# Splitting the projection of v over the two row halves of TensorE

## The chip, the cores and the metric

The kernel runs on one core of a Trainium2 chip. The metric is the time of one execution on the device, in microseconds; lower is better. The engines are TensorE (PE, with its weight loads as PEld), VectorE (DVE), ScalarE (ACT), GpSimd (POOL) and SyncE (SP), which issues transfers.

## The reference

With S = 2048 rows, D = 512, 32 heads of 16 and 688 gate channels, the kernel computes, from `xn = layernorm(x)`, the sum of `x` and two branches:

```
q, k, v = split(xn @ wqkv)                        # 32 heads of 16
pq, pk  = q @ w_phi, k @ w_phi                    # per head
phi(p)  = concat(softmax(p), softmax(-p))         # 32 features per head
kv, z   = phi(pk)^T v, sum over s of phi(pk)
o       = (phi(pq) kv) / (phi(pq) z + 1e-6)
A       = o @ wo

y       = gelu(xn @ w_in)                         # 2 x 688 channels
z1, z2  = y[:688], layernorm(y[688:])
B       = (z1 * (w_sp @ z2 + b_sp)) @ w_out

out     = x + A + B
```

## The kernel before, in words

All matmul products of accuracy are made of three: each operand is split into a high part `h` (rounded to the type float32r) and a rest `l`, and `mm3` adds `ah bh`, `ah bl` and `al bh` into the same PSUM bank (lines 51, 52, 53).

The first stage goes over 16 tiles of 128 rows of x. For a tile `s` the rows are centred, transposed on TensorE (`transposed`, line 248, into a tile `pt`) and split into `xT[s]`, whose first 512 columns in each of two slices hold the high part and the rest, as four chunks of 128 contraction rows by 128 tokens. Then there are three projections from the same `xT[s]`: `proj_k` and `proj_q` (weights folded with the feature map beforehand, in the matmuls `fold` of line 197) and `proj_v`. Each is `proj`: four chunks of three matmuls with 128 contraction rows, 128 output partitions and 512 columns, all into one PSUM tile named `proj`, which is one bank. k and q go through `softmax_pair`: four VectorE operations that read `proj` (lines 103, 104, 108, 109), an exponential on ScalarE (line 110), a sum and a reciprocal (lines 112, 113). v is evacuated by one ScalarE activation that scales each row (line 257). `add_kv` (lines 267 to 274) multiplies the features of k (line 269) and accumulates `kvps`, 16 small matmuls per tile of 32 output partitions and 64 columns, each of two instructions, over all 16 tiles.

The PSUM tiles of this stage are `kv_ps` with 2 banks, `za` with 2 and `p0ps` with 4 (tag "mm"); the 4 are shared by `proj` of k, q and v and by the transposes. v has two buffers in SBUF, so v of tile s + 2 is written when `kvps` of tile s has read its own. While the stage runs, matmuls named `zps` (two sums of twelve matmuls with 344 columns per tile) make the gate's first half (`z1_raw`, lines 136 to 140); they use the banks of `za`.

The order of the first two tiles is written out by hand (lines 296 to 339: `keep` puts an instruction into the order of its engine). From tile 0's `add_kv` on, the loop of line 341 gives an order of priority only: `proj_k(s)`, the transposes of `s + 2`, `proj_q`, `add_kv(s)`, `proj_v(s + 2)`, then `zps`. A planner that simulates the engines puts every engine's instructions in order, and may bring forward later work whose inputs are ready. On the chip each engine then keeps to that order.

Later stages make the second half of the gate, the large product with `w_sp` (matmuls named `g`), and the output: `po` (line 761, 64 output partitions, 256 columns) and `pout`.

Of the kernel before, what the change touches and what calls it, by code (L numbers as in the profile page):

```python
# [10 lines left out]
F32 = mybir.dt.float32  # L11
F32R = mybir.dt.float32r
AF = mybir.ActivationFunctionType
ALU = mybir.AluOpType
# [4 lines left out]
P = 128  # L19
S, D, H, DH, FH = 2048, 512, 32, 16, 688  # L20
NT = S // P
ND = D // P
# [9 lines left out]
HP, QP = P // 2, P // 4  # L32
# [3 lines left out]
def mixer(ctx: ExitStack, tc: tile.TileContext, x, x_t, wv, wqkT, phi_bd, wo, w_in, wst, b_r, w_out, out):  # L36
    nc = tc.nc
    pe, act, dve, pool, sp = nc.tensor, nc.scalar, nc.vector, nc.gpsimd, nc.sync
# [10 lines left out]
    def mm3(dst, a, b, start, stop):  # L49
        (ah, al), (bh, bl) = a, b  # L50
        pe.matmul(dst, ah, bh, start=start, stop=False)  # L51
        pe.matmul(dst, ah, bl, start=False, stop=False)  # L52
        return pe.matmul(dst, al, bh, start=False, stop=stop).ins  # L53
# [25 lines left out]
    r_x = cst.tile([P, NT], F32, name="r_x")  # L79
# [42 lines left out]
    def zproj(ps, s, w, order=(0, 1)):  # L122

        if ps in (za, kv_ps_p):
            p = [ps.tile([P, D], F32, tag="z", name="zps") for _ in range(2)]
        else:
            q = ps.tile([P, 2, D], F32, tag="z", name="zps")
            p = [q[:, k] for k in range(2)]
        t = xT[s]
        for k, j in enumerate(order):  # L130
            for c in range(ND):
                cs = slice(c * P, (c + 1) * P)
                mm3(p[k][:, :FC], (t[:, 0, cs], t[:, 1, cs]), (w[j][0][:, c], w[j][1][:, c]), c == 0, c == ND - 1)
        return [(slice(k, k + 1), p[k][:, :FC].unsqueeze(1)) for k in range(2)] if ps in (za, kv_ps_p) else [(slice(0, 2), q[:, :, :FC])]
# [8 lines left out]
    xT = []  # L143
# [17 lines left out]
    with ExitStack() as p0:  # L161
        res = p0.enter_context(left("p0res", 1))
        wk = p0.enter_context(left("p0wk", 2))
        ps = p0.enter_context(psum("p0ps", 4))
# [6 lines left out]
        wv_h = res.tile([P, ND, D], F32R, name="wv_h")  # L171
        wv_l = res.tile([P, ND, D], F32R, name="wv_l")
# [40 lines left out]
        def proj(s, wh, wl):  # L213
            p = ps.tile([P, D], F32, tag="mm", name="proj")
            for c in range(ND):
                cs = slice(c * P, (c + 1) * P)
                proj.last = mm3(p, (xT[s][:, 0, cs], xT[s][:, 1, cs]), (wh[:, c], wl[:, c]), c == 0, c == ND - 1)
            return p

        xt, v = {}, {}  # L220

        def fetch(s):
# [31 lines left out]

        def proj_v(s):
            v[s] = wk.tile([P, D], F32, tag="v", name="v")
            ins = act.activation(v[s], proj(s, wv_h, wv_l), AF.Copy, scale=r_x[:, s:s + 1]).ins
            return proj.last, ins

        def proj_k(s):  # L260
# [35 lines left out]
        with ExitStack() as queue:  # L296
# [22 lines left out]
            p = proj(0, wqk_h[:, 1], wqk_l[:, 1])  # L319
# [6 lines left out]
            keep(dve=i, act=center(2, nm))  # L326
            ek = softmax_pair(wk, p, "k", r_x[:, 0:1])
            keep(pe=proj_v(0)[0])
            for k in range(2):
                accs = [(2 * k + m, za.tile([P, D], F32, tag="z", name="fold")) for m in range(2)]  # L330
                for g in range(NG):
                    i = fold(wqT, g, accs)
                folded(0, accs)
                if k == 0:
                    keep(pe=i)
                    pt, i = transposed(2)
                    keep(pe=i)
                    split_x(pt)
                    proj_v(1)
        n1 = nq = 0  # L340
        for s in range(NT):
            fetch(s + 4)
            er = proj_k(s) if s else ek
            if 0 < s < NT - 2:
                centered(s + 2)
            while nq < (s - 2) * NT // (NT - 3):
                proj_q(nq)
                nq += 1
            add_kv(s, er)
            if s + 2 < NT:  # L350
                proj_v(s + 2)
            if s == 1:
                for j in range(2):
                    load_win(w1[j], j, wk, "x", XB)
            while n1 < s * (NT - LAG) // (NT - 1):
                z1_raw(wk, za, n1, 2)
                n1 += 1
# [18 lines left out]
    def q_fin(et, tmp, zb):  # L376

        e, r, t, w = et[:, :NF], *(et[:, NF + k * 2 * H:NF + (k + 1) * 2 * H] for k in range(3))
        den = et[:, NF + 6 * H:QW]
        dve.tensor_tensor(tmp, e, zb, op=ALU.mult)  # L380
        dve.tensor_reduce(t, heads(tmp), axis=AX.X, op=ALU.add)
        dve.tensor_tensor(t, t, r, op=ALU.mult)
        dve.scalar_tensor_tensor(den, pairs(t, 0), EPS_DEN, pairs(t, 1), op0=ALU.add, op1=ALU.add)
        dve.reciprocal(den, den)
        dve.tensor_tensor(w.rearrange("p (h a) -> p h a", a=2), r.rearrange("p (h a) -> p h a", a=2),
                          den.unsqueeze(2).to_broadcast([P, H, 2]), op=ALU.mult)
        return e, dve.tensor_tensor(heads(e), heads(e), bc(w, 2 * H), op=ALU.mult).ins
# [46 lines left out]
    with ExitStack() as p1:  # L434
# [39 lines left out]
        for s in range(NE):  # L474
            et = load_q(s, tb.tile([P, QW], F32, tag="et", bufs=2, name="et"))
            tmp = zw.tile([P, 4, FC], F32, tag="z2", bufs=2, name="qtmp").rearrange("p a b -> p (a b)")[:, :NF]
            e, _ = q_fin(et, tmp, zb)
# [56 lines left out]
    for s in range(NT):  # L534
        p = zproj((kv_ps_p, zc, zbp, za)[s % 4], s, w2, (0, 1) if s % 2 == 0 else (1, 0))
# [4 lines left out]
        for k, q in p:  # L540
            ins = act.activation(z[:, k], q, AF.Gelu_apprx_tanh, scale=r_x[:, s:s + 1]).ins
# [6 lines left out]
        r = zw.tile([P, 1], F32, tag="rstd", bufs=2, name="rstd")  # L548
# [206 lines left out]
    def attend(fs):  # L755

        oT = [wk.tile([P, NG, 2 * P], F32R, tag=f"oT{k}", name="oT") for k in "hl"]
        po = [pso.tile([P, 2, 2 * P], F32, tag="po", bufs=2, name="po") for _ in range(2)]
        for g in range(NG):
            for a in range(2):  # L760
                lasts[3] = pe.matmul(po[g // 2][a * HP:(a + 1) * HP, g % 2], kvT[:, 2 * g + a], fs[g][:, a],  # L761
                                     start=True, stop=True).ins
        for k in range(2):
            gs = slice(2 * k, 2 * k + 2)
            round_h(act, oT[0][:, gs], po[k])
            ins = rest_l(oT[1][:, gs], po[k], oT[0][:, gs])
        return oT, ins

    def project_u(i, u):
        uh, ul, rt = u  # L770
        p = pso.tile([P, D], F32, tag="out", bufs=2, name="pout")
        for c in range(KF):
            mm3(p, (uh[:, c], ul[:, c]), wu[c], c == 0, False)
        for w in wu[KF]:
            pe.matmul(p, rt, w, start=False, stop=False)
        return p
# [13 lines left out]
    p = {0: project_u(0, uT.pop(0))}  # L790
# [5 lines left out]
    oT, ins = attend(fT)  # L796
# [14 lines left out]
    for i in range(0, NT, 2):  # L811
        if i:
# [3 lines left out]
            with tc.issue_after(lasts[2]):  # L816
                oT, _ = attend(fT)
# [49 lines left out]
```

## Time and profile before

| | |
|---|---|
| time, median of 2 runs | 655.19 us (654.72 and 655.67) |
| span of the profiled execution | 651.5 us |
| time of the profiled execution outside its span | not given by the profile; the median is 3.7 us above the span |
| TensorE busy | 644.0 us, 99% of the span |
| VectorE busy | 509.3 us, 78% |
| ScalarE busy | 279.4 us, 43% |
| first stage with its 16 tiles | to about 215 us of the span |

A row of the groups of instructions gives line, engine, operation, written tile <- read tiles, shapes and count, then busy time and mean duration in ns, then idle time ahead of it and its cause. The duration of a matmul runs from its start to the end of its passage through the array; consecutive matmuls overlap, so what one costs in a dense stretch is the distance between two starts. In the chain of work that ended last, the second number of a row is the time that the step added to the chain. A row of waits gives what waited, for whom, the microseconds in total, the number of times and the longest. In the forms, `128*64` is the number of array rows and columns that a matmul uses.

### The profile page before, as it was taken

The page shows a single profiled execution, that of the slowest core. Times are in us where ns is not written, and L with a number is a line of the kernel's source. Part 1 is how long each engine was busy: PE and PEld are TensorE (multiplying, and loading weights), DVE is VectorE, ACT ScalarE, POOL GpSimd, SP SyncE. Part 2 cuts the span into 40 slices and gives each one's busy share as a digit, 9 for nine tenths or more (in the row PEclk, how much of TensorE's full clock was granted, in tenths as well). Part 3 has the DMA queues.
Part 4 walks back from the last instruction along what each step waited for, and adds up shares of the span by engine and source line. Part 5 has one row for each costly group of instructions (what it writes and reads, how often), then busy time and mean ns, then how long its engine had stood idle before and what let it go on. Part 6 is the DMA issues. An engine that isn't in the chain of part 4 may idle for free.

```text
span 651.5 us, 10927 instructions
## 1 busy us (share of the span) xinstructions
PE 644.0 (99%) x4163; PEld 580.2 (89%) x4163; DVE 509.3 (78%) x921; ACT 279.4 (43%) x464; POOL 96.6 (15%) x185
## 2 busy tenths in 40 slices
PE   7999999999999999999999999999999999999997
PEld 6888888888888999999999999999999777787885
DVE  4988987998889578989977869678696588989321
ACT  5644334342333438887443434434452432233220
POOL 3332221101101014441010010010100000001000
PEclk9999999999999999999999999999999999999999
DMA  8365344544444951002353352433557867864610
GB/s 307 78 161 138 100 130 103 149 124 113 124 141 144 302 164 65 2 2 78 129 187 128 124 171 89 163 122 115 177 182 269 290 210 265 295 237 165 214 50 32
DMA packets 38884, 98.36 MB, mean 151 GB/s; under 512 B 4688, under 2 KB 6736, under 8 KB 38832
## 3 DMA queue, kind: packets, MB, share of 16 engines
q1 hardware_dynamic: 27632, 56.77, 26.7%
q0 software_dynamic: 8896, 35.26, 17.8%
q10 hardware_dynamic: 2304, 5.64, 2.3%
q8 instruction: 32, 0.52, 0.3%
q14 instruction: 20, 0.16, 0.1%
HBM read 56.37 MB, written 26.61 MB: 127 GB/s over the span
## 4 chain that ended last, share of the span: by engine, by line
PE 97%; DMA 1%; DVE 0%; ACT 0%; SPq 0%; issue 0%; POOL 0%; POOLq 0%
PE g L53 11%; PE g L52 11%; PE g L51 11%; PE proj L53 7%; PE proj L51 7%; PE proj L52 7%; PE zps L53 6%; PE zps L52 6%; PE zps L51 6%; PE pout L51 5%; PE pout L53 5%; PE pout L52 5%; PE po L761 2%; PE kvps L273 1%; PE ptq L749 1%; PE pt L248 1%
## 5 line engine op out<-in xcount | busy, mean ns | idle before, releaser
L53 PE MATMUL g<-B,A 128*128 128x344 f32 x448 | 143.3, 320 | 0.0
L52 PE MATMUL g<-B,A 128*128 128x344 f32 x448 | 143.2, 320 | 0.0
L51 PE MATMUL g<-B,A 128*128 128x344 f32 x448 | 143.2, 320 | 0.0
L51 PEld LDWEIGHTS g<-B,A 128*128 128x128 f32 x448 | 84.2, 188 | 0.0
L53 PEld LDWEIGHTS g<-B,A 128*128 128x128 f32 x448 | 84.2, 188 | 0.0
L52 PEld LDWEIGHTS g<-B,A 128*128 128x128 f32 x448 | 84.1, 188 | 0.0
L47 DVE TENSOR_TENSOR A<-S,A 128x512 fp32r<-128x512 f32 x64 | 43.7, 688 | 33.4 <-ACT A L43 32.5
L43 ACT ACTIVATE A<-S 128x512 fp32r<-128x512 f32 x64 | 40.0, 631 | 58.5 <-PE g L53 36.3
L110 ACT ACTIVATE e<-e,r_x 128x1024 f32<-128x1024 f32 x32 | 36.8, 1152 | 43.8 <-DVE e L109 43.1
L51 PE MATMUL proj<-wqk_h,xT 128*128 128x512 f32 x128 | 51.4, 401 | 0.3 <-ACT wqk_h L43 0.3
L52 PE MATMUL proj<-wqk_l,xT 128*128 128x512 f32 x128 | 50.5, 394 | 1.1 <-DVE wqk_l L47 1.1
L43 ACT ACTIVATE A<-wf 128x512 fp32r<-128x512 f32 x64 | 33.4, 522 | 41.1 <-PE g L53 40.4
L53 PE MATMUL proj<-wqk_h,xT 128*128 128x512 f32 x128 | 50.9, 397 | 0.0
L51 PE MATMUL zps<-w_0h,xT 128*128 128x344 f32 x128 | 41.8, 326 | 0.0
L112 DVE TENSOR_REDUCE sm<-e 128x64 f32<-128x1024 f32 x32 | 38.6, 1208 | 3.3 <-ACT e L110 3.3
L53 PE MATMUL zps<-w_0h,xT 128*128 128x344 f32 x128 | 41.1, 321 | 0.0
L51 PE MATMUL zps<-w_1h,xT 128*128 128x344 f32 x128 | 41.0, 320 | 0.0
L53 PE MATMUL zps<-w_1h,xT 128*128 128x344 f32 x128 | 41.0, 320 | 0.0
L52 PE MATMUL zps<-w_0l,xT 128*128 128x344 f32 x128 | 40.9, 320 | 0.0
L52 PE MATMUL zps<-w_1l,xT 128*128 128x344 f32 x128 | 40.9, 319 | 0.0
L47 DVE TENSOR_TENSOR A<-wf,A 128x512 fp32r<-128x512 f32 x64 | 35.4, 553 | 3.9 <-ACT A L43 3.4
L751 ACT ACTIVATE f<-ptq 128x512 f32<-128x512 f32 x32 | 16.5, 603 | 34.7 <-PE ptq L749 27.8
(193 smaller groups left out, 1439.9 us busy)
## 6 DMA issues: line engine op xcount, KB each, us to landing
wf<-in_wst SPq DMA_DIRECT2D x64, 256.0 KB, 3.4
e_d<-e POOLq DMA_DIRECT2D x16, 544.0 KB, 5.2
et<-e_d SPq DMA_DIRECT2D x16, 544.0 KB, 4.9
zacc<-e POOLq DMA_DIRECT2D x16, 512.0 KB, 4.9
er<-et POOLq DMA_DIRECT2D x12, 512.0 KB, 4.6
u_d<-z1t POOLq DMA_DIRECT2D x16, 368.0 KB, 4.4
u<-u_d SPq DMA_DIRECT2D x15, 368.0 KB, 4.6
z_d<-z1f ACTq DMA_DIRECT2D x16, 344.0 KB, 3.4
```

Of the source, the lines that this page charges most:

```text
L43: return act.activation(h, src, AF.Copy).ins
L47: return (eng or dve).tensor_tensor(l, src, h.bitcast(F32), op=ALU.subtract).ins
L51: pe.matmul(dst, ah, bh, start=start, stop=False)
L52: pe.matmul(dst, ah, bl, start=False, stop=False)
L53: return pe.matmul(dst, al, bh, start=False, stop=stop).ins
L110: act.activation(e, e, AF.Exp, scale=scale)
L112: dve.tensor_reduce(sm, heads(e), axis=AX.X, op=ALU.add)
L248: ins = pe.transpose(pt[:, c], xs[:, c * P:(c + 1) * P], ident).ins
L273: pe.matmul(kv_acc[k:k + QP, m // 4], vs[:, m * QP:(m + 1) * QP], e[:, m * HP:(m + 1) * HP], start=s == 0 and m < 4, stop=s == NT - 1, ski ...
L749: pe.transpose(pt[:, a, k].bitcast(F32R), src, ident_r)
L751: act.activation(f, pt.rearrange("p a k b -> p a (k b)"), AF.Copy)
L761: lasts[3] = pe.matmul(po[g // 2][a * HP:(a + 1) * HP, g % 2], kvT[:, 2 * g + a], fs[g][:, a], start=True, stop=True).ins
```

## The change

`proj_v` no longer calls `proj`. A new function `proj_rows` takes two PSUM tiles from the same four banks. Each of the 12 matmuls of the projection becomes two, one over contraction rows 0 to 63 and one over rows 64 to 127 of the same chunk (`HP` is 64), which write one bank each; the two alternate. ScalarE evacuates the first bank into v with the row scale, as before. A new VectorE operation multiplies the second bank by the same scale and adds v, in place. `proj.last` is the last matmul of either kind, and the instruction that `proj_v` returns for the evacuation is now the VectorE one. The projections of k and q stay as they are.

```diff
+        def proj_rows(s, wh, wl):
+            p = [ps.tile([P, D], F32, tag="mm", name="projr") for _ in range(2)]
+            for c in range(ND):
+                cs = slice(c * P, (c + 1) * P)
+                for k, (a, b) in enumerate(((0, wh), (0, wl), (1, wh))):
+                    for r in range(2):
+                        rows = slice(r * HP, (r + 1) * HP)
+                        proj.last = pe.matmul(p[r], xT[s][rows, a, cs], b[rows, c], start=c == 0 and k == 0,
+                                              stop=c == ND - 1 and k == 2).ins
+            return p
+
         def proj_v(s):
             v[s] = wk.tile([P, D], F32, tag="v", name="v")
-            ins = act.activation(v[s], proj(s, wv_h, wv_l), AF.Copy, scale=r_x[:, s:s + 1]).ins
+            r = r_x[:, s:s + 1]
+            p = proj_rows(s, wv_h, wv_l)
+            act.activation(v[s], p[0], AF.Copy, scale=r)
+            ins = dve.scalar_tensor_tensor(v[s], p[1], r, v[s], op0=ALU.mult, op1=ALU.add).ins
             return proj.last, ins
```

## The prediction

> **What bounds the kernel now.** First the page: busy shares, the granted clock, and the chain that ended last.
>
> ```profile
> PE 644.0 (99%) x4163; PEld 580.2 (89%) x4163; DVE 509.3 (78%) x921; ACT 279.4 (43%) x464; POOL 96.6 (15%) x185
> ...
> PEclk9999999999999999999999999999999999999999
> ...
> PE 97%; DMA 1%; DVE 0%; ACT 0%; SPq 0%; issue 0%; POOL 0%; POOLq 0%
> ```
>
> TensorE holds 97% of the chain, at a granted clock of nine tenths or more in every slice (1.00 in the table of stretches below). A nanosecond more of TensorE time is a nanosecond of the kernel, and work elsewhere costs only where TensorE comes to wait for it. The change touches the first stage alone; the table of stretches shows that stage.
>
> ```profile
> core 0: us, PE busy (x) PEld busy (x) DVE busy (x) ACT busy (x) POOL busy (x), PEclk, DMA share, GB/s
> ...
> 20.00:30.00 10.00, 10.00 (x54) 8.59 (x55) 10.00 (x19) 8.18 (x15) 3.03 (x10) 1.00 0.29 81
> ...
> 70.00:80.00 10.00, 10.00 (x78) 8.10 (x77) 9.93 (x17) 4.74 (x6) 2.33 (x5) 1.00 0.50 136
> ...
> 120.00:130.00 10.00, 10.00 (x77) 7.98 (x76) 9.93 (x16) 3.64 (x5) 2.53 (x5) 1.00 0.25 47
> 130.00:140.00 10.00, 10.00 (x80) 8.26 (x79) 9.97 (x15) 3.55 (x5) 1.43 (x2) 1.00 0.53 148
> ...
> 20.00:205.00 185.00, 185.00 (x1345) 155.37 (x1346) 162.16 (x245) 77.16 (x105) 36.55 (x69) 1.00 0.46 126
> ```
>
> From 20 to 205 us TensorE is busy in all 185.00 us. VectorE is idle for 185.00 - 162.16 = 22.8 us of it, but in four of the ten-microsecond stretches for under 0.1 us: it is the near second. ScalarE has over 100 us to spare. Who waits in this stage:
>
> ```profile
> DVE mm L103 <- PE proj L53: 9.6, 11, 2.1
> DVE st L234 <- DMA xt<-in_x: 7.7, 4, 2.7
> DVE sm L112 <- ACT e L110: 2.7, 3, 1.6
> ...
> ACT v L257 <- PE kvps L273: 10.3, 7, 2.3
> ```
>
> VectorE waits for TensorE, not the other way; the evacuation of v on ScalarE waits, in 7 of 16 cases, for `kvps` to give back a buffer of v. That wait will matter below.
>
> **The change, part by part.** What it takes away: 16 projections of 12 matmuls. Forms first, then one projection by its start times.
>
> ```profile
> L51 PEld LDWEIGHTS proj<-wv_h,xT x64: 186/188/192, 15.0 to 185.5; 128*128 128x128 f32 x64
> L51 PE MATMUL proj<-wv_h,xT x64: 387/392/505, 15.0 to 185.7; 128*128 128x512 f32 x64
> L52 PE MATMUL proj<-wv_l,xT x64: 387/394/398, 15.3 to 185.9; 128*128 128x512 f32 x64
> L53 PE MATMUL proj<-wv_h,xT x64: 389/392/497, 15.5 to 186.2; 128*128 128x512 f32 x64
> L257 ACT ACTIVATE v<-proj,r_x x16: 665/687/697, 19.8 to 192.9; 128x512 f32<-128x512 f32 x16
> ```
>
> ```profile
> 108.72 0.32 PE L51 MATMUL zps<-w_1h,xT 128*128 128x344 f32 x1
> ...
> 110.61 0.39 PE L51 MATMUL proj<-wqk_h,xT 128*128 128x512 f32 x1
> ...
> 158.21 0.40 PE L51 MATMUL proj<-wv_h,xT 128*128 128x512 f32 x1
> ...
> 160.98 0.32 PE L51 MATMUL zps<-w_1h,xT 128*128 128x344 f32 x1
> ```
>
> A matmul lasts 392 ns but they overlap: 12 start between 158.21 and 160.98, so a step is 2.77 / 12 = 0.231 us. Twelve of 344 columns take 110.61 - 108.72 = 1.89 us, 0.1575 each. The difference, 0.0735 us for 168 columns, is 0.4375 ns per column: 512 columns stream for 0.224 us, and 0.007 us a step is left that does not depend on the columns. All of v costs 192 x 0.231 = 44.4 us of the path.
>
> What it adds on TensorE: 384 matmuls over 64 rows, each still streaming 512 columns, alternately into two banks. **If a pair of halves runs side by side, a pair costs what one matmul costs now; if not, twice that.** No matmul over half of the rows is in this trace. The nearest rows are the matmuls over part of the columns, 32 (`kvps`) and 64 (`po`). Forms, then their steps in the chain:
>
> ```profile
> L273 PE MATMUL kvps<-e,v x512: 219/219/244, 31.0 to 214.8; 128*32 128x64 f32 x171
> ...
> L761 PE MATMUL po<-f,kvT x128: 379/379/431, 513.4 to 637.5; 128*64 128x256 f32 x128
> ```
>
> ```profile
> 26.59 1.78 PE fold L197 x16
> ...
> 61.72 0.58 PE kvps L273 x32
> 62.30 0.43 PE proj L51
> 62.73 0.23 PE proj L52
> ...
> 564.88 1.88 PE po L761 x16
> 566.76 0.43 PE pout L51
> 567.19 0.24 PE pout L52
> ```
>
> `fold` is full-array and of the same plain float kind, 128 columns: 1.78 / 16 = 0.111 us each, one after another. At that rate 32 `kvps` of 64 columns would take 32 x 0.0556 = 1.78 us; they take 0.58. Sixteen `po` of 256 columns would take 16 x 0.2225 = 3.56 us; they take 1.88. So parts of the array do run side by side here, four and two at a time. I take the same for rows: 192 pairs at 0.231 us, a change of **0**. Bounds: gain of the fixed part, 192 x 0.007 = -1.3 us; loss with no overlap, 192 x 0.231 = +44.4 us.
>
> The Trainium skill ("TensorE: Matmul & The Clock Gate", The mechanism, in Part 3) says that a weight load overlaps running matmuls only when the row groups differ. By that rule the halves would hide loads which are now exposed, and the pairs would be quicker. The trace disagrees: the load lasts 188 ns, and a step leaves 7 ns beyond its columns. The same page (Measured speedup vs the span model) has 3.07 times for four row tiles instead of 4; an estimate from that share would make a pair 0.231 / 0.77 = 0.30 us, 13 us over 192 pairs, and would bring the sum below to 675. No run here shows row tiles.
>
> Second, the **way into and out of the divided array**. The same rows price it. Eight rounds of four `kvps` stream for 8 x 0.0556 = 0.445 us and take 0.58; the first full matmul behind them takes 0.43 instead of 0.23. That is 0.135 + 0.20 = 0.335 us per excursion. For `po`: 8 pairs stream for 1.78 us and take 1.88, then 0.43 again: 0.30. Two different divisions, one price; I take 0.32. In the timeline the 192 matmuls of v stand in 21 unbroken runs, because the planner puts `zps` matmuls into some projections; first and last matmul:
>
> ```profile
> 15.00 0.47 PE L51 MATMUL proj<-wv_h,xT 128*128 128x512 f32 x1
> ...
> 186.15 0.39 PE L53 MATMUL proj<-wv_h,xT 128*128 128x512 f32 x1
> ```
>
> 21 x 0.32 = **+6.7 us**, in full on the path. Bounds: 0, if rows are divided without emptying the array; 32 runs, two per projection, x 0.335 = 10.7 us. The Trainium skill ("TensorEngine Tiling (Array Packing)", Key Properties) says that a change of tiling mode drains the engine; that the trace agrees for columns is the 0.32 us, for rows no run here shows it.
>
> Third, **VectorE**: 16 operations more, two inputs of 128x512, one from PSUM. Nearest rows:
>
> ```profile
> L594 DVE SCALAR_TENSOR_TENSOR c<-g,bias,c 128x344 f32<-128x344 f32 x32 | 17.7, 568 | 1.0 <-PE g L53 0.4
> ...
> L784 DVE TENSOR_TENSOR xr<-pout,xr 128x512 f32<-128x512 f32 x16 | 11.0, 689 | 17.1 <-PE pout L53 17.0
> ```
>
> The same operation on 344 columns is 568 ns, a two-input one of this size 689 ns. 16 x 0.69 = 11.0 us (bounds: 16 x 0.568 = 9.1, and in proportion to the columns 16 x 0.845 = 13.5). All are below VectorE's 22.8 us of idle time, under TensorE's work, so **0** on the path; if that cover is gone, up to 13.5 us. Two of the adds belong to the opening, where VectorE is full from 20 to 30 us; they push its queue 1.4 us back, under the second fold and the projections after it. ScalarE still evacuates one bank per tile: no change. No DMA is added, so SP and POOL have nothing new.
>
> Fourth, **waits and banks**. The new add waits for ScalarE, which waits for `kvps`. Behind the add, in order, stand the reductions and subtractions of the next softmax (L103 to L109), and for these waits ScalarE's exponential, then `kvps`. The pool has 4 banks; a tile took one each for k, q, the transpose and v, now v takes two and the second goes free one VectorE operation later. How long v holds a bank:
>
> ```profile
> 66.68 0.39 PE L51 MATMUL proj<-wv_h,xT 128*128 128x512 f32 x1
> ...
> 75.80 0.69 ACT L257 ACTIVATE v<-proj,r_x 128x512 f32<-128x512 f32 x1 [1.75 <-PE kvps L273]
> ```
>
> From the first matmul to the end of the evacuation: 9.8 us, most of the (192.9 - 19.8) / 15 = 11.5 us from one v to the next (row of L257). Two of four banks then belong to v for much of the time. `zps` has banks of its own and can fill the gaps, so I take 0; the price without that cover is among the rivals.
>
> **Sum.** The shown runs have a median of 655.19 us; the span is 651.5, and the profile gives no time of its own execution beyond it, so 3.7 us lie around it. Stage: 0 + 6.7 + 0 + 0 = +6.7, span 658.2, time 655.19 + 6.7 = 661.9; I say **662**, 1.0% slower and so inside the 2% (642.1 to 668.3) that a measurement of this kernel can hardly tell from no change.
>
> **The rivals.** (1) *Halves don't run side by side*, so the change does the opposite of what its form says. For it: no row halves in this trace, and each pair writes two banks on the same 128 partitions, where `kvps` and `po` write different partitions. Against: the column cases overlap fully. It decides from the first pair that starts 0.23 us instead of some ns after its partner. 44.4 us more than the sum: 699 to 706.
> (2) *VectorE and the banks become the bound.* One place: the new add holds v's second bank until VectorE reaches it, and TensorE waits for a bank. For it: the stretches with under 0.1 us of idle time. Against: 22.8 us over the stage. It decides where the add, 0.69 us, exceeds the 1.4 us that VectorE idles per tile on average (22.8 / 16) less what the waits eat. Half to all of 13.5 us on top of the sum: 669 to 676.
> (3) *Halves are nearly free to enter, or hide the load's rest* (the skill's rule above). The 0.007 us a step is all there is: -1.3 us plus up to 8 excursions (2.6 us), with half a microsecond of spread between runs 653 to 657: not slower.
>
> **How the numbers follow.** The forecast, 657 to 668, gets 0.55; (1) 0.16, as nothing here shows row halves; (2) 0.17; (3) 0.11; 0.01 is left for a gain over 2%, for which 13 of v's 44.4 us would have to vanish. The range runs from (3) through (2), 653 to 676, and leaves (1) out. Slower by over 2%: (1) and (2), 0.33; within: 0.55 + 0.11 = 0.66; faster: 0.01.
>
> **What would show it.** Right: the two halves of a pair start within some 10 ns and pairs step by 0.22 to 0.24 us; the first full matmul behind a run of halves shows 0.43 in the chain; VectorE busy grows by 9 to 14 us with no TensorE wait in the stage. Wrong: pairs stepping by 0.46 us; or rows in which TensorE's `projr` or `proj` waits for VectorE; or a planner that cuts v into other than about 21 runs, which moves the sum by 0.32 us each.

## The result and the profile after

The changed kernel takes 687.31 us (median of 2 runs, 685.69 to 688.93) against 655.19: a ratio of 1.0496, 95% interval 1.0465 to 1.0527, or 32 us more. The forecast was 662 us with a range of 653 to 676. The profiled execution spans 687.2 us.

The page of the changed kernel, the same three lines as before:

```profile
PE 667.4 (97%) x4355; PEld 587.6 (86%) x4355; DVE 522.1 (76%) x937; ACT 278.5 (41%) x464; POOL 96.1 (14%) x185
...
PEclk9989999999999989999999999999999999999999
...
PE 88%; DVE 5%; DMA 5%; issue 1%; ACT 0%; SPq 0%; POOL 0%; DVEq 0%
```

VectorE is busy for 12.8 us more, as forecast. TensorE is busy for 23 us more, and 9% of the chain has gone over to VectorE and DMA: TensorE now waits, and the clock has two slices under nine tenths. By the starts of the matmuls the loss lies ahead of the product `g`: its first matmul comes at 291.1 us of the span before and at 323.5 after, 32.4 later. The span as a whole grew by 35.7. The other 3 us are a wait of 1.7 us for a load of `u` behind `g` and a slower clock from 538.3 to 541.7 us, in stages that the change doesn't touch; the other execution of the changed kernel has a span of 684.0.

Inside the changed stage, the starts in the timeline around one projection of the changed kernel (start, duration, line, form):

```profile
156.92 0.40 PE L53 MATMUL proj<-wqk_h,xT 128*128 128x512 f32 x1
157.24 0.50 PE L227 MATMUL projr<-wv_h,xT 64*128 64x512 f32 x1
157.59 0.39 PE L227 MATMUL projr<-wv_l,xT 64*128 64x512 f32 x1
157.91 0.42 PE L51 MATMUL zps<-w_1h,xT 128*128 128x344 f32 x1
158.18 0.31 PE L52 MATMUL zps<-w_1l,xT 128*128 128x344 f32 x1
...
160.62 0.39 PE L227 MATMUL projr<-wv_l,xT 64*128 64x512 f32 x2
160.85 0.62 PE L227 MATMUL projr<-wv_h,xT 64*128 64x512 f32 x4
161.31 0.39 PE L227 MATMUL projr<-wv_l,xT 64*128 64x512 f32 x2
```

Three things are to be seen. First the way in and out: the four steps are 0.32, 0.35, 0.32 and 0.27 us, where 0.231, 0.231, 0.231 and 0.157 would do without a change of division: 0.09 + 0.12 + 0.09 + 0.11 = 0.41 us. Second, these two halves are **alone**: both belong to one half of the rows, and their partners run later, alone too. Third, where both partners are there, they run side by side: the last three rows begin three pairs in the 0.69 us from 160.62 to 161.31, 0.23 us a pair, and in the trace the two of a pair start 3 to 4 ns apart. Over the stage the 384 halves occupy 221 steps where 192 would do, and stand in 34 unbroken runs, where v had 21 before.

Who made TensorE wait up to `g`, then the stage and three stretches of time (columns as before):

```profile
PE projr L227 <- ACT xT L43: 5.4, 1, 5.4
PE kvps L287 <- DVE e L283: 2.8, 1, 2.8
PE zps L51 <- DVE e L109: 1.4, 1, 1.4
PE proj L52 <- DVE wqk_l L47: 1.1, 1, 1.1
PE pt L259 <- DVE e L109: 0.9, 1, 0.9
```

```profile
20.00:237.00 217.00, 210.77 (x1538) 165.98 (x1537) 173.72 (x260) 76.53 (x106) 35.24 (x69) 0.98 0.39 107
38.00:44.00 6.00, 0.64 (x5) 0.35 (x5) 4.53 (x10) 2.06 (x4) 1.92 (x6) 0.95 0.35 124
43.00:52.00 9.00, 8.20 (x34) 5.68 (x34) 5.27 (x8) 3.38 (x6) 2.80 (x6) 0.62 0.29 76
236.00:252.00 16.00, 11.76 (x109) 10.24 (x108) 11.53 (x18) 4.55 (x7) 3.34 (x5) 0.79 0.90 252
```

Of these waits only the 1.1 us for `wqk_l` stood in the trace of before. TensorE does almost nothing from 38 to 44 us, and then has a granted clock of 0.62 from 43 to 52; the last tile's waits near 240 us are followed by the same. The chain shows how the first of them came about:

```profile
36.69 2.76 DMA xt<-in_x
...
40.09 0.73 DVE v L271
40.82 0.60 DVE st L245
...
43.27 0.49 ACT xT L43
43.76 0.04 issue
43.80 1.22 PE projr L227 x4
...
46.17 0.43 PE proj L53
46.60 0.43 PE proj L51
```

A load of x lands late, VectorE does the new add (40.09) ahead of that tile's statistics, ScalarE centres the rows and only then writes the `xT` for which the next projection waits. After that pause a full matmul steps by 0.43 us in place of 0.23.

An account of the 32.4 us from these readings: 34 ways in and out at 0.40 us, less 0.2 for each of the 11 ends that adjoin `kvps` and change the division anyway, 11.4; 29 steps more at 0.231, 6.7; the four pauses of TensorE that before did not have, 11; matmuls at the slower clock behind two of them, 5. That is 34, 2 more than there are. Readings of one trace prove no cause; the experiments below take the terms apart.

### The profile page after: what moved, and what is told of

Same layout as the page of the kernel before. It is cut to its first block, busy times and chain, and to the rows that moved or that the text cites. A ratio compares the mean times of both kernels' runs of the same rounds, so it can differ in the third digit from the quotient of the medians.

```text
span 687.2 us, 11360 instructions
## 1 busy us (share of the span) xinstructions
PE 667.4 (97%) x4355; PEld 587.6 (86%) x4355; DVE 522.1 (76%) x937; ACT 278.5 (41%) x464; POOL 96.1 (14%) x185
## 4 chain that ended last, share of the span: by engine, by line
PE 88%; DVE 5%; DMA 5%; issue 1%; ACT 0%; SPq 0%; POOL 0%; DVEq 0%
PE g L53 10%; PE g L52 10%; PE g L51 10%; PE projr L227 6%; PE zps L51 6%; PE zps L52 6%; PE zps L53 6%; PE pout L51 5%; PE pout L52 5%; PE pout L53 5%; PE proj L51 4%; PE proj L52 4%; PE proj L53 3%; PE po L775 2%; PE ptq L763 1%; DMA xt<-in_x 1%
## 5 line engine op out<-in xcount | busy, mean ns | idle before, releaser
L227 PE MATMUL projr<-wv_h,xT 64*128 64x512 f32 x256 | 53.6, 417 | 5.4 <-ACT xT L43 5.4
L51 PE MATMUL proj<-wqk_h,xT 128*128 128x512 f32 x128 | 52.8, 413 | 0.3 <-ACT wqk_h L43 0.3
L53 PE MATMUL proj<-wqk_h,xT 128*128 128x512 f32 x128 | 51.3, 400 | 0.0
L227 PEld LDWEIGHTS projr<-wv_h,xT 64*128 64x128 f32 x256 | 30.2, 187 | 17.2 <-ACT xT L43 5.6
L51 PE MATMUL zps<-w_0h,xT 128*128 128x344 f32 x128 | 43.1, 336 | 1.4 <-DVE e L109 1.4
L53 PE MATMUL zps<-w_0h,xT 128*128 128x344 f32 x128 | 41.8, 327 | 0.0
```

What stands on the lines that cost most here:

```text
L227: proj.last = pe.matmul(p[r], xT[s][rows, a, cs], b[rows, c], start=c == 0 and k == 0, stop=c == ND - 1 and k == 2).ins
```

## The experiments

Every kernel was timed in three rounds beside the kernel before, whose median was 653.9 to 654.9 us in the four groups. Differences below are to the kernel before of the same group. Theory A is that the divided array costs (ways in and out, lone halves); theory B that the second bank, held until VectorE reaches it, makes TensorE wait.

### Two banks without halves

```diff
-  (halves of rows into p[0] and p[1])
+  r = c // 2
+  proj.last = mm3(p[r], (xT[s][:, 0, cs], xT[s][:, 1, cs]), (wh[:, c], wl[:, c]), c % 2 == 0, c % 2 == 1)
```

> The second bank and the VectorE add alone: full-array matmuls, chunks 0 and 1 into one bank, 2 and 3 into the other, evacuated as in the changed kernel. Theory A (the divided array costs: 34 ways in and out at about 0.40 us, and 29 steps in which a half runs alone, 0.23 us each): 655 to 658 us. Theory B (a second bank held until VectorE reaches it makes TensorE wait, and idle TensorE loses its clock): 668 to 678 us. If both, 658 to 668.

Measured: 668.33 us, 14.4 more; ratio 1.0209 (1.0193 to 1.0226). No row half is in this kernel. So theory A alone falls: a loss of 14 us, at the lower edge of theory B's range, needs no division of the array. Waits of TensorE, and of ScalarE for v, in this kernel:

```profile
PE kvps L284 <- DVE e L280: 5.9, 1, 5.9
PE proj L51 <- ACT v L267: 1.7, 2, 0.9
PE kvps L284 <- ACT e L110: 1.5, 1, 1.5
...
ACT v L267 <- PE kvps L284: 8.6, 8, 4.2
```

The 5.9 us are at the last tile: VectorE has fallen behind, and the last `kvps` waits for its features. Only 1.7 us are waits of TensorE for the bank itself. The starts of the matmuls show where the rest comes from. While projections are held up, `zps` is brought forward: when `kvps` of the thirteenth of 16 tiles starts, at 191 us, 288 `zps` matmuls are done, and no other one starts until the last `kvps`. Before, at the same tile, it was 207. From there on nothing fills TensorE's gaps, and all of its new waits lie behind 191 us. `zps` didn't cover the hold, it put its price off. In the changed kernel the same 288 are reached at the fifteenth `kvps`, at 238 us, where its waits at the last tile begin.

### The add alone, and the second bank alone

```diff
+  act.activation(v[s], proj(s, wv_h, wv_l), AF.Copy, scale=r_x[:, s:s + 1])
+  ins = dve.scalar_tensor_tensor(v[s], v[s], 1.0, v[s], op0=ALU.mult, op1=ALU.max).ins
```

> The kernel before with one VectorE operation more per tile, on v in SBUF after its evacuation (the larger of v and v), no second bank, no halves. If VectorE's extra work is what the full-array run with two banks paid for: 664 to 669 us, with TensorE waiting for VectorE at the last tile. If the second bank is: 655 to 657 us.

Measured: 654.98 us, 0.3 more; 1.0007 (0.9997 to 1.0017). VectorE's extra work by itself (16 operations of 0.68 us) costs nothing.

```diff
-  ins = dve.scalar_tensor_tensor(v[s], p[1], r, v[s], op0=ALU.mult, op1=ALU.add).ins
   (full-array matmuls into two banks)
```

> Full-array matmuls into two banks without the add; the second bank (chunks 2 and 3) is left out of v. If the second bank is what cost 14 us: 662 to 668 us. If VectorE's work is: 654 to 657 us.

Measured: 656.15 us, 1.4 more; 1.0021 (1.0011 to 1.0030). The second bank by itself costs 1.4 us. Neither part is the 14 us: the remaining 13 come only when the add has to free the bank.

### A third buffer of v

The add follows ScalarE's evacuation, which with two buffers of v follows `kvps` of two tiles before.

```diff
-  v[s] = wk.tile([P, D], F32, tag="v", name="v")
+  v[s] = wk.tile([P, D], F32, tag="v", bufs=3, name="v")
```

> The run with full-array matmuls in two banks and the VectorE add, with three buffers of v. If the second bank is held because the evacuations wait for a buffer of v: 655 to 659 us. If it is held because VectorE is late of itself: 665 to 670 us, as with two buffers.

Measured, on the kernel with full-array matmuls, two banks and the add: 656.44 us, 1.6 more; 1.0024 (1.0014 to 1.0035). Of the 14 us 12 to 13 are gone, and so are TensorE's new waits; 209 `zps` are done at the thirteenth `kvps`, much as before, and ScalarE's wait for v is now for the projection itself:

```profile
ACT v L267 <- PE projr L53: 7.0, 7, 1.3
```

So with full arrays theory B holds, with its cause: the bank is held through the chain `kvps`, ScalarE, VectorE. The control:

> The kernel before with three buffers of v: its evacuation waited 10.3 us for them, off TensorE's path. No change, 653 to 656 us.

Measured: 654.47 us; 0.9994 (0.9985 to 1.0003), no change. The third buffer helps only where the second bank waits.

> The changed kernel with three buffers of v instead of two, so that neither evacuation waits for the sums of two tiles before. If halves run alone because the banks wait for a buffer of v: fewer than 10 lone steps and fewer ways in and out, 668 to 676 us. If the planner cuts the projection for another reason: 680 to 690 us.

Measured, on the changed kernel: 682.4 us, 27.7 more; 1.0426 (1.0410 to 1.0441). Only 4 to 5 us less than the changed kernel, 33 runs and 224 steps. The waits at the last tile are gone, the wait of 5.3 us near 40 us is not. So in the changed kernel this hold is worth 4 to 5 us, not the 12 to 13 of the full-array version. The lone halves have another cause, and 28 us remain.

### Halves without the add

```diff
-  act.activation(v[s], p[0], AF.Copy, scale=r)
-  ins = dve.scalar_tensor_tensor(v[s], p[1], r, v[s], op0=ALU.mult, op1=ALU.add).ins
+  ins = act.activation(v[s], p[0], AF.Copy, scale=r).ins
```

> Row halves without the VectorE add; the second bank is left out of v and goes free when its last matmul ends. Theory A: the ways in and out and some lone halves stay, 667 to 676 us. Theory B: most of the 32 us goes, 656 to 664 us.

Measured: 679.38 us, 25.4 more; 1.0384 (1.0366 to 1.0402). Beside the full-array run with the second bank and no add (1.4 more), the halves alone cost 24 us. Theory B alone falls too, and theory A's range ended 3 us lower. Its trace has 27 runs (10.4 us by the price above, two ends shared), 23 steps over 192 (5.3 us) and 6.5 us of new waits, 4.3 of them near 40 us with a slower clock behind them.

### The way in and out alone

```diff
   p = ps.tile([P, D], F32, tag="mm", name="proj")
+  pe.matmul(p[:, :HP], xT[s][:HP, 0, :P], wh[:HP, 0, :HP], start=True, stop=True)   # for v alone
```

> The kernel before with one more matmul ahead of each projection of v, over 64 rows and 64 columns into the same bank, overwritten by the projection: 16 ways into a row half and out again, no second bank, no add. Theory A: 16 x 0.40 = 6.4 us more, 660 to 663 us. If a way in and out is what I took from the column cases, 0.32, it is 5.1 us: 660. If it costs next to nothing for rows: 655 to 656 us.

Measured: 660.66 us, 6.7 more; 1.0100 (1.0083 to 1.0117): 0.42 us each for 16, of which 0.03 is the matmul itself (64 columns at 0.4375 ns). One of them in its timeline:

```profile
68.81 0.32 PE L53 MATMUL zps<-w_0h,xT 128*128 128x344 f32 x1
69.06 0.29 PE L216 MATMUL proj<-wv_h,xT 64*128 64x64 f32 x1
69.28 0.50 PE L51 MATMUL proj<-wv_h,xT 128*128 128x512 f32 x1
69.62 0.40 PE L52 MATMUL proj<-wv_l,xT 128*128 128x512 f32 x1
```

From 68.81 to 69.62 are 0.81 us, where 0.157 + 0.231 + 0.03 = 0.42 would do: 0.39 us. The price of a change of division is shown by itself, without a second bank or VectorE; what in the array takes this time is not shown.

### Fewer cuts

These are two attempts to keep the halves together. The first puts the 24 matmuls into a section that the planner treats as one:

```diff
+  with tc.tile_critical() if s > 1 else ExitStack():
       (the loops of proj_rows)
```

> The changed kernel with the 24 matmuls of a projection kept together from the third tile on, so that no half runs alone and there are about 17 ways in and out instead of 34. Theory A: 17 x 0.4 = 7 us and what is left of the stalls, 663 to 671 us. Theory B: the projection now starts only when both banks are free, so waits stay or grow, 676 to 690 us.

Measured: 708.06 us, 54.1 more; 1.0822 (1.0783 to 1.0861). That is outside both ranges, and it settles nothing about the cuts: 16 runs remained, but the start of most projections is 0.8 to 2.4 us behind the matmul ahead of it, because the section as a whole waits for other engines. Three of those waits:

```profile
PE projr L228 <- DVE e L108: 2.8, 1, 2.8
PE projr L228 <- issue: 2.5, 3, 1.6
...
PE projr L228 <- POOL r_x L85: 2.4, 2, 2.0
```

The row scales on POOL, for one, are no operand of these matmuls.

The second turns the three products round. In the built programs a projection is cut behind its first two products, because the third needs the rest of x, which VectorE writes later than ScalarE writes the high part.

```diff
-  enumerate(((0, wh), (0, wl), (1, wh)))
+  enumerate(((1, wh), (0, wh), (0, wl)))
```

> The changed kernel with the order of the three products turned round: the one with the rest of x, whose operand VectorE writes last, goes first. In the built program the 384 matmuls of v then stand in 23 unbroken runs instead of 34. If the ways in and out and the lone halves are what the halves cost (0.42 us each, measured; 0.23 us each): 11 x 0.42 = 4.6 us less and up to 6.7 us less, 675 to 682 us. If the cost lies in stalls that do not depend on the cuts: 684 to 690 us.

Measured: 683.14 us, 28.7 more; 1.0440 (1.0420 to 1.0460). 3 to 4 us less than the changed kernel, between the two ranges, so neither was met: 23 runs and 206 steps instead of 34 and 221, but 14 of the ends adjoin `kvps` and saved nothing, and TensorE's new waits grew from 10.5 to 15.0 us.

### Both banks in one tile

```diff
-  ps = p0.enter_context(psum("p0ps", 4))
+  ps = p0.enter_context(psum("p0ps", 2))
-  p = [ps.tile([P, D], F32, tag="mm", name="projr") for _ in range(2)]
+  q = ps.tile([P, 2, D], F32, tag="vv", bufs=1, name="projr")
+  p = [q[:, r] for r in range(2)]
```

The control has the full-array loop of the first experiment in place of the halves; the third version has the product with the rest of x first.

> The control: full-array matmuls with chunks 0 and 1 in one bank and 2 and 3 in the other, both banks one tile of a pool of their own, two banks left for k, q and the transposes, ScalarE and the VectorE add as in the changed kernel. Two banks fewer for the rest: 660 to 680 us, as TensorE waits for banks.

> The changed kernel with both banks of v as one tile of a pool of its own (two banks for v, two for k, q and the transposes), so that they go free together: 29 runs in the built program, no lone halves. Against its control (the same banks with full-array matmuls) 29 x 0.42 = 12 us more, if ways in and out are all that is left; 18 us or more above the control, if something else about halves costs.

> Halves with both banks in one tile and the product with the rest of x first: 20 runs, no lone halves. 20 x 0.42 = 8.4 us above the control with full-array matmuls, and 9 x 0.42 = 3.8 us below the same without the turned order. If the cuts do not matter: the same time as that.

Measured: control 673.94 us (19.5 more), halves 682.10 (27.6 more), halves with the rest first 680.59 (26.1 more). Here no half runs alone: 192 steps in both. The halves are 8.2 and 6.7 us above their control, less than the 12 and 8.4 expected. 29 and 20 runs at 0.40 us, less 0.2 for the 15 ends next to `kvps` in each, a deduction made after the result, give 8.6 and 5.0. The two versions with halves are not told apart: ratios of 1.0431 (1.0414 to 1.0448) and 1.0404 (1.0383 to 1.0425) overlap. So once halves are paired, ways in and out account for what they cost here to within 2 us. It is not a pure comparison: TensorE's waits sum to 14 us in all three, but 4 of them lie near 40 us with halves and not in the control.

### One half after the other

```diff
-  for c in range(ND): ... for k, (a, b) in ...: for r in range(2):
+  for r in range(2): for c in range(ND): ... for k, (a, b) in ...:
```

> The changed kernel with all twelve matmuls of the first half ahead of the twelve of the second, so that partners cannot start together. If pairs do run side by side in the changed kernel, at about 0.23 us a pair, this adds 160 to 190 steps of 0.23 us: 715 to 735 us. If the halves were one after another there too: 685 to 692 us.

Measured: 709.56 us, 54.8 more; 1.0830 (1.0812 to 1.0848). That is between the two ranges, 22 us above the changed kernel. The halves take 353 distinct starts here, and a run of halves of one kind steps by 0.23 us, but the planner mixed the second kind into the first at some tiles, where halves started 0.11 us apart and still overlapped. So a lone half costs a full step, and the exact price of all-lone halves was not measured.

### Halves without the other causes

```diff
+  if s < 4:
+      ins = act.activation(v[s], proj(s, wv_h, wv_l), AF.Copy, scale=r).ins
+      return proj.last, ins
```

> The changed kernel with the projections of tiles 0 to 3 as before (full array, one bank, no add) and halves from tile 4 on. If the stall of 5.4 us near 40 us of the span and the slower clock behind it come from halves in the opening: both gone, 670 to 677 us. If they come from the order of the loads and not from the halves: 680 to 686 us.

Measured: 668.06 us, 13.2 more; 1.0209 (1.0179 to 1.0239): 19 us less than the changed kernel for four tiles out of sixteen, 2 us below the first range. The pause near 40 us and the slow clock behind it are gone. So are, which was not expected, the slow clock at the last tile and most of the waits there: 2.4 us of new waits are left in all. Its trace has 27 runs of halves, and v takes 205 steps (48 of them full-array).

With the rest first and three buffers of v as well:

> Halves from tile 4 on, the product with the rest of x first, three buffers of v: in the built program each of the 12 divided projections is one unbroken run of 24. If only the ways in and out are left: 12 x 0.40 = 4.8 us above the kernel before, 658 to 662 us. If the second bank with the add goes on costing 10 us: 668 to 674 us.

Measured: 663.16 us, 8.3 more; 1.0124 (1.0101 to 1.0146), just above what was expected from 12 ways in and out alone. Each divided projection is one run; one of them:

```profile
151.02 0.32 PE L53 MATMUL zps<-w_1h,xT 128*128 128x344 f32 x1
151.27 0.73 PE L227 MATMUL projr<-wv_h,xT 64*128 64x512 f32 x4
...
153.90 0.40 PE L227 MATMUL projr<-wv_l,xT 64*128 64x512 f32 x2
154.23 0.50 PE L51 MATMUL proj<-wqk_h,xT 128*128 128x512 f32 x1
154.56 0.40 PE L52 MATMUL proj<-wqk_l,xT 128*128 128x512 f32 x1
```

From 151.27 to 154.23 are 2.96 us for 12 pairs, 0.19 more than 12 x 0.231; that is the second step and the first full matmul behind the pairs, each 0.10 late in the trace: **a pair of halves costs what one full matmul cost**. The rest of the 8.3 us over 4.8 is about as long as the new waits of TensorE, 3.9 us ahead of four `kvps`. No kernel tried here beats the one before.

## Why the prediction was wrong, step by step

*Halves run side by side, 192 pairs at 0.231 us, change 0.* Right: the row above, and the controls in one tile. The rival in which they don't (699 to 706) is excluded as a mechanism, though the time came out between it and the forecast.

*Ways in and out, 21 x 0.32 = 6.7 us.* Right as a mechanism, mis-sized in both factors: 34 runs, and 0.39 to 0.42 us. The price came from the column cases, 0.10 to 0.135 us inside the division and 0.20 behind it; with rows it is 0.09 on the way in, 0.12 at the second step and 0.20 on the way out. The count was taken from the order of before, and the order changes with the operation: a bank that comes free by itself and a rest of x that comes late each make one more run. With the ends shared with `kvps` taken off, about 11 us instead of 6.7.

Rival 3, in which the way in is nearly free, falls with this.

*Partners always start together.* This was assumed, not costed. 29 lone steps, 6.7 us. With both banks in one tile, which go free together, there were none; that fits a planner that issues one half ahead of the other when its bank is free first.

*VectorE's 11 us are covered.* Right by itself: 0.3 us for 16 operations of 0.68 us on SBUF alone.

*Waits and banks, 0.* **This is the step that failed**, and with it the weighing of rival 2. In place of 0 the trace of the changed kernel has 10.5 us of new waits of TensorE ahead of `g`, and about 5 us of matmuls at half the clock behind them. One part of it is the hold of the second bank. I read the hold rightly in the trace of before, but took `zps` for a cover; with full arrays `zps` runs out at 191 us, and the kernel loses 14.4 us, just above the highest price of that rival (13.5). I set the rival beside the forecast as an alternative, where both can hold at once: 6.7 and 13.5 together would have given 675. That is still 12 us short, and the prices overlap: in the changed kernel the hold is worth 4 to 5 us (the run with three buffers of v). Of the signs of being wrong that the prediction names, one showed, 34 runs for 21. The new waits of TensorE for VectorE are those of `zps`, `kvps` and `pt`, not of `projr` or `proj`.

*What was not in the sum at all*, and is the other part of that step: the pause near 40 us, 5.4 us, and TensorE's slower clock after it, about 3 us. Taking halves out of the opening removed both, with a part of the ways in and out, the second bank and the add in four tiles, and most of the waits at the last tile, for 19 us together; the price of the pause alone was not measured. That the pause comes with halves in the opening is shown: seven kernels with them wait there for 3.4 to 6.5 us, the one without the add among them, and no run with full arrays does. The kernel with `tile_critical` alone has halves there and no such pause. Why the planner's order runs dry there is open; that it prices a pair of halves as two matmuls, and so expects TensorE later than it comes, would fit and was not tested.

The Trainium skill ("TensorEngine Tiling (Array Packing)", Key Properties) says that a change of division empties the array. For rows the runs agree in that the change costs 0.4 us here; the emptying itself is not seen. The estimate from the table of the Trainium skill ("TensorE: Matmul & The Clock Gate", Measured speedup vs the span model), that a stream of pairs loses as four row tiles do, does not hold here: 0.23 us a pair, not 0.30.

## What to carry to other kernels

Dividing the array buys nothing where the full array was already in use: the columns streamed stay the same, and each excursion cost 0.4 us here, so keep divided matmuls in few unbroken runs. Before giving a tile a second PSUM bank, follow who frees it, through the SBUF buffer that the evacuation waits for: here one more buffer of 128x512 was worth 12 to 13 us in the full-array version, and 4 to 5 in the one with halves. Work that fills a gap early is missing later: count how long it lasts before calling it a cover. And rivals that can hold at the same time belong into one sum, though their prices may overlap.

## What the runs showed of the hardware

After a pause of TensorE of 5.4 us, matmuls of 512 columns stepped by 0.43 us instead of 0.23 from about 44 to 50 us, at a granted clock of 0.50 (0.62 over the stretch from 43 to 52); the same came at the last tile behind waits of 2.8 and 1.4 us, from 241.3 to 248.2, and behind the wait of 1.7 us in the output, from 538.3 to 541.7. The stretches at half the clock are 6.83, 6.83 and 3.41 us long, and in the other traces of this case, where they lie inside the kernel, 3.41, 6.83 or 10.24: one, two or three times 3.41 us. Not every pause has one: behind a wait of 1.9 us at 77 us of the last kernel above, the clock stayed at 1.00. The Trainium skill ("TensorE: Matmul & The Clock Gate", What's actually happening) gives half rate after an idle window of about 3.4 us and full rate after a busy one; the trace agrees on the half rate and on the length of a window, but in the output a wait of 1.7 us was enough. What a pause costs besides its length depends on where the slow stretch falls: near 40 us in the changed kernel it began 0.4 us before the pause ended and cost about 3 us more; in the full-array run with two banks it began at 218.8 us, 3.3 us before the pause ended, so 3.5 us of it fell on matmuls.
